# Attention scores of both heads of a pair together, as three float32r products of split queries and keys

## The chip, the core and the metric

The kernel runs on one core of one Trainium2 chip. The metric is the device time of one execution in microseconds (us). The core's engines work side by side, each through its own list in order: TensorE (PE) multiplies matrices into PSUM, VectorE (DVE) and ScalarE (ACT) do elementwise work and read PSUM, GpSimd (POOL) does elementwise work in SBUF, and SyncE (SP) issues the DMA transfers. Semaphores hold them together.

## The reference

Attention with a position bias made by a small network, for 2 batches, 8 heads, 576 positions and 64 columns a head; then two feed-forward layers over the 1152 rows of 512 columns.

```python
scores = scale * np.matmul(q, k.transpose(0, 1, 3, 2))      # scale = 1/8
x = (log1p(|i - j|) / log1p(max(i, 1)))[..., None]
bias = np.maximum(x @ w1 + b1, 0.0) @ w2                    # hidden 32, one column per head
scores = scores + bias.transpose(2, 0, 1)[None]
attn = softmax(scores)                                      # over the last axis
x = (attn @ v), heads side by side: (1152, 512)
h = x @ w_in;  x = (h * np.clip(h + 3.0, 0.0, 6.0) / 6.0) @ w_out       # d_ff 2048
xn = x / sqrt(mean(x * x) + 1e-06) * rms_g
x = (silu(xn @ w_gate) * (xn @ w_val)) @ w_out2                         # d_ff 1536
```

## The kernel before

**Tiles and units.** The 1152 query rows are nine tiles of 128. Eight tiles lie in one batch each; the seventh (`COMB`) holds the last 64 rows of both batches. A tile has four units `u`, one for each pair of heads, so there are 36 units; unit `u` is pair `u % 4` of tile `u // 4`.

**A unit.** `scores` (L418) is called once for each head `a` of the pair. Keys and queries lie transposed with 64 columns of a head on 64 partitions, even positions of the keys in the upper row half and odd ones in the lower half, and the queries are there twice, so a head is two fp32 matmuls of 128 queries by 288 keys (`L427`), one on each row half, into the two banks of one PSUM tile `s`. (The combined tile takes 64 queries for each batch: four matmuls.) The profile has two records for each fp32 matmul, the order one. `softmax_d` (L441, VectorE) adds the bias and takes the maximum `m`; `softmax_a` (L452, ScalarE) does the exponential. `e_turn` transposes the weights `e` in three parts, four, four and one blocks, on PE (`tps`), `e_copy` (L472) copies each part from PSUM to `et`, and `pv` (L490) multiplies with the values, ten fp32 matmuls. Once a tile the sums are inverted (`ri`), spread (`rb`), transposed (`rps`) and copied (`rt`, L514); `xf` (L519) applies them, and `xh` (a rounding to float32r, L528) and `xl` (what is left, L526) are the two parts that the feed-forward phases read. `k_copy` (L315) and `q_copy` (L325) bring transposed keys and queries from PSUM to SBUF.

**Bias.** It depends on the position alone. For each of 36 groups of 16 rows, `bias_R` (L344, L339) makes four tiles `R`, `bias_mm` (L357) contracts them on PE (`bps`), `bias_evac` brings them to `ev`, and `bias_store` (L387) writes them to DRAM; `bias_load` (L413, L410) reads a unit's bias back shifted, once the eight groups of its rows are stored. The groups are spread over the first twenty units or so.

**Feed-forward.** Weights, activations and normed rows are split into a float32r part and the rest, and every product is three float32r matmuls (`PASS`): L701 for the first product, L746 for the second. A weight is loaded by SP into `raw`, and turned into its two parts by ScalarE (`wm`, `wh`), VectorE (L138, L139, L143) and GpSimd (`wl`), one step a turn. A first few are converted while attention still runs, into `nb` early slots.

**What sets the order.** Each piece of work has a key, a number in units of `u`, made from `PARAMS`; the pieces are emitted in the order of their keys. Those up to key `man` keep that order on each engine; the later ones go through a scheduler, which orders each engine's list within what buffers and dependences allow. `START`, `MID`, `ET`, `KE` and `RB, RT, XH, XL` say on which engine (P, A, D) a copy is done. `BUFS` has the number of buffers of each pool: the score tiles `s` have two of two PSUM banks each, which wide bias products use too (L348). In the feed-forward part the order is the program's.

## Time and profile before

| | us |
|---|---|
| median of 3 runs (lowest to highest) | 662.5 (660.59 to 663.89) |
| the profiled execution | 662.26 |
| its span | 660.5 |
| busy: PE, VectorE, ScalarE, GpSimd | 633.3, 479.8, 342.6, 144.7 |

The span is what the trace shows; the profiled execution's own time has some 1.8 us around it. Busy time is the union of an engine's instructions, and matmuls are pipelined, so a PE that is busy all the time need not be at its peak; a share over the whole span is a mean of stages with different limits. In the trace attention ends at 218.2 us, where the first feed-forward matmul starts.

### The profile page before, as it was taken

The page shows a single profiled execution, that of the slowest core. Times are in us where ns is not written, and L with a number is a line of the kernel's source. Part 1 is how long each engine was busy: PE and PEld are TensorE (multiplying, and loading weights), DVE is VectorE, ACT ScalarE, POOL GpSimd, SP SyncE. Part 2 cuts the span into 40 slices and gives each one's busy share as a digit, 9 for nine tenths or more (in the row PEclk, how much of TensorE's full clock was granted, in tenths as well). Part 3 has the DMA queues.
Part 4 walks back from the last instruction along what each step waited for, and adds up shares of the span by engine and source line. Part 5 has one row for each costly group of instructions (what it writes and reads, how often), then busy time and mean ns, then how long its engine had stood idle before and what let it go on. Part 6 is the DMA issues. An engine that isn't in the chain of part 4 may idle for free.

```text
span 660.5 us, 11012 instructions
## 1 busy us (share of the span) xinstructions
PE 633.3 (96%) x4174; PEld 525.0 (79%) x4174; DVE 479.8 (73%) x885; ACT 342.6 (52%) x675; POOL 144.7 (22%) x117
## 2 busy tenths in 40 slices
...
GB/s 153 282 287 239 266 164 261 131 80 204 140 3 1 55 139 133 127 126 126 128 64 1 33 96 128 143 149 129 153 160 65 79 114 1 63 153 230 34 0 49
DMA packets 75250, 80.69 MB, mean 122 GB/s; under 512 B 23996, under 2 KB 59964, under 8 KB 75196
## 3 DMA queue, kind: packets, MB, share of 16 engines
...
q8 instruction: 33, 0.54, 0.3%
...
## 4 chain that ended last, share of the span: by engine, by line
PE 80%; DVE 11%; DMA 3%; issue 3%; ACT 1%; SPq 1%; DVEq 0%; ACTq 0%
PE h L701 33%; PE ya L746 16%; PE yb L746 8%; PE pv L490 6%; PE tps L86 6%; PE s L427 6%; PE bps L357 4%; DVE wm L139 2%; DVE e L441 1%; DVE wm L143 1%; DVE wm L138 1%; DMA bias<-biasd 1%; PE qps L86 1%; DMA raw<-in_moe_w_out_dram 1%; DVE R L344 1%
## 5 line engine op out<-in xcount | busy, mean ns | idle before, releaser
L151 POOL TENSOR_TENSOR wl<-wm,wh 128x512 fp32r<-128x512 f32 x86 | 126.4, 1470 | 301.1 <-ACT wh L122 176.2
L143 DVE SCALAR_TENSOR_TENSOR wm<-raw,wm 128x512 int32<-128x512 int32 x86 | 127.5, 1482 | 0.9
L710 ACT CAST gh<-r 128x384 fp32r<-128x384 f32 x84 | 43.2, 514 | 118.0 <-DVE r L733 71.2
L701 PE MATMUL h<-nh,wh 128*128 128x384 f32 x288 | 97.6, 339 | 5.1 <-DVE r L733 3.2
L701 PE MATMUL h<-nh,wl 128*128 128x384 f32 x288 | 96.7, 336 | 0.0
L701 PE MATMUL h<-nl,wh 128*128 128x384 f32 x288 | 96.5, 335 | 0.0
L441 DVE CUSTOM_DVE_ANT_1 e<-s,bias 128x576 f32<-128x576 f32 x72 | 54.3, 755 | 29.8 <-PE tps L86 17.7
L733 DVE TENSOR_TENSOR r<-r,h 128x384 f32<-128x384 f32 x36 | 19.9, 551 | 66.6 <-PE h L701 66.3
L452 ACT ACTIVATE e<-e,m 128x576 f32<-128x576 f32 x72 | 56.0, 778 | 19.8 <-DVE m L441 19.8
L701 PE MATMUL h<-xh,wh 128*128 128x384 f32 x192 | 65.4, 341 | 0.0
L701 PE MATMUL h<-xh,wl 128*128 128x384 f32 x192 | 64.7, 337 | 0.0
L139 DVE SCALAR_TENSOR_TENSOR wm<-raw,wm 128x512 int32<-128x512 int32 x86 | 62.5, 727 | 2.9
L701 PE MATMUL h<-xl,wh 128*128 128x384 f32 x192 | 64.4, 336 | 0.0
L701 PEld LDWEIGHTS h<-nh,wh 128*128 128x128 f32 x288 | 54.1, 188 | 8.6 <-DVE r L733 4.0
L130 ACT ACTIVATE wm<-raw 128x512 f32<-128x512 f32 x86 | 58.0, 674 | 5.1 <-DMA raw<-in_moe_w_in_dram 2.2
L713 DVE TENSOR_TENSOR gl<-r,gh 128x384 fp32r<-128x384 f32 x84 | 46.6, 554 | 15.6 <-ACT gh L710 15.6
L427 PE MATMUL s<-kS,q 64*128 64x288 f32 (+1 forms) x320 | 54.6, 449 | 2.7 <-DVE m L441 2.7
L86 PEld LDWEIGHTS tps<-ident,e 128*128 128x128 f32 x324 | 42.5, 200 | 18.2 <-issue 8.9
L86 PE MATMUL tps<-ident,e 128*128 128x128 f32 x324 | 55.9, 297 | 0.1
L344 DVE TENSOR_SCALAR R<-T,NB 128x368 f32<-128x368 f32 (+17 forms) x124 | 54.0, 485 | 2.2 <-PE bps L357 1.7
L122 ACT CAST wh<-wm 128x512 fp32r<-128x512 f32 x86 | 52.9, 617 | 4.7 <-DVE wm L143 4.7
L701 PEld LDWEIGHTS h<-nl,wh 128*128 128x128 f32 x288 | 54.1, 188 | 1.4
...
## 6 DMA issues: line engine op xcount, KB each, us to landing
...
```

Source lines behind the costliest of these rows:

```text
L86: nc.tensor.transpose(out, in_, ident[:n, :n])
L122: nc.scalar.copy(out=hi, in_=m)
L130: nc.scalar.activation(out=m, in_=raw[:, :, 1].bitcast(F32), func=ACTF.Abs, scale=2.0 ** -112)
L139: nc.vector.scalar_tensor_tensor(out=m, in0=raw[:, :, 0], scalar=29, in1=m, op0=ALU.logical_shift_right, op1=ALU.bitwise_or,)
L143: nc.vector.scalar_tensor_tensor(out=m, in0=raw[:, :, 1], scalar=-0x80000000, in1=m, op0=ALU.bitwise_and, op1=ALU.bitwise_or,)
L151: nc.gpsimd.tensor_tensor(out=lo, in0=m, in1=hi, op=ALU.subtract)
L344: nc.vector.tensor_scalar(out=R, in0=src, scalar1=NB1[:, col], scalar2=None, op0=ALU.max)
L427: nc.tensor.matmul(s[sl, r, :SH], lhsT=q_t[t][h // 4][rows, h % 4, sl], rhs=kS[b][rows, h, :], start=True, stop=True,)
L441: nc.vector.tensor_tensor_reduce(out=e_t[u][:, a, :].rearrange("p (j r) -> p r j", r=2), in0=s[:, :, :SH], in1=bt[u][:, a, :].rearrange("p ...
L452: nc.scalar.activation(out=e_t[u][:, a, :], in_=e_t[u][:, a, :], func=ACTF.Exp, scale=-1.0, bias=m_t[t][:, h:h + 1], accum_out=sum_t[t][:, ...
L701: nc.tensor.matmul(ps, lhsT=w[wz][:, c * 128:(c + 1) * 128], rhs=x[xz][:, c, :], start=(i == 0), stop=(i == 11),)
L746: nc.tensor.matmul(y_t[ph, n, t], lhsT=g[gz][:, t * 128:(t + 1) * 128], rhs=w[wz], start=(f == 0 and i == 0), stop=(f == F - 1 and i == 2),)
```

## The change

Keys and queries are each split into a float32r part (`h`) and the rest (`l`), on the way out of PSUM: `k_part` and `q_part` take the places of `k_copy` and `q_copy`, once for the high part (the engine of before, now a cast) and once for the low part (VectorE: a subtraction that reads PSUM again). A score is three products, high by high, high query by low key, low query by high key, which add up in PSUM. `scores` is called once a unit and emits both heads. In the combined tile the queries of each batch get tiles of their own with zeros in the other batch's 64 columns, so that all matmuls have 128 queries and both batches add into one tile: twelve matmuls a head. The numbers in `PARAMS` move keys: bias groups come closer together (`gr` 1.076 to 1.163), bias loads are asked earlier (`bl` -3.209 to -5.532), one block of k is asked 2.3 units earlier (`k4` -0.333 to -2.61), the values of both batches are loaded closer together (`lv0`, `lv1`), and `kl` and `ql`, 0.1 and 0.3 units, set the low parts behind the high ones. The engine strings move copies: for each fourth unit the first part-1 copy of `et` and for each fourth the one-block copy go from VectorE to ScalarE, `rt` and `xh` too, and `xl` goes from GpSimd to VectorE. Six early weight slots stand in place of eight, nine `R` buffers in place of eleven, three `ev` in place of four. `far` has the value that stood in the code.

```diff
--- before.py
+++ after.py
@@ -27,22 +27,22 @@
-    g0=-5.972, gs=0.601, g8=-0.524, gt=-0.138, g14=1.055, gr=1.076, man=-0.96, zra=-0.531, zrd=-0.393, zrp=-1.107,
+    g0=-5.972, gs=0.601, g8=-0.524, gt=-0.138, g14=1.055, gr=1.163, man=-0.96, zra=-0.643, zrd=-0.393, zrp=-1.107,
...
 START = ["DDDD", "DDAA", "DDAD", "DDDA", "DDDD", "DDDA", "DDDA", "DDDD"]
 MID = ["DDDD", "DDDA"]
-ET = ["DADA", "DAAA", "DDDD"]
+ET = ["DADA", "AAAA", "DADD"]
 KE = ["D", "D"]
-RB, RT, XH, XL = "PDDP"
-SLOTS = dict(wr=3, na=0, nb=8, ns=29)
-BUFS = dict(rawk=4, rawq=2, qp=2, bp=5, ep=2, etp=3, sm=3, Rp=11, evp=4, xa=1, ps_s=2, ps_t=3, ps_v=1)
+RB, RT, XH, XL = "PAAD"
+SLOTS = dict(wr=3, na=0, nb=6, ns=29, far=60)
+BUFS = dict(rawk=4, rawq=2, qp=2, bp=5, ep=2, etp=3, sm=3, Rp=9, evp=3, xa=1, ps_s=2, ps_t=3, ps_v=1)
 
 
 @with_exitstack
@@ -80,6 +80,9 @@
 
     xh = [xp.tile([128, 4, BT], F32R, tag=f"xh{n}", name=f"xh{n}") for n in range(NB)]
     xl = [xp.tile([128, 4, BT], F32R, tag=f"xl{n}", name=f"xl{n}") for n in range(NB)]
+
+
+    PASS = ((0, 0), (0, 1), (1, 0))
 
     def transpose(out, in_):
         n = in_.shape[0]
@@ -247,7 +250,7 @@
         ps_v = actx.enter_context(tc.tile_pool(name="ps_v", bufs=BUFS["ps_v"], space=PSUM))
 
 
-        kS = [p.tile([128, H, SH], F32, name=f"kS{b}") for b, p in enumerate((kp0, kp1))]
+        kS = [[p.tile([128, H, SH], F32R, name=f"kS{b}{z}") for z in "hl"] for b, p in enumerate((kp0, kp1))]
         vs = [p.tile([128, 2, H, 2, D], F32, name=f"vs{b}") for b, p in enumerate((vp0, vp1))]
 
         v4 = [p.tile([128, 4, 2, D], F32, name=f"v4{b}") for b, p in enumerate((vp0, vp1))]
@@ -304,25 +307,40 @@
         def k_turn(x):
             ps_of["k", x] = turn_four(raw_t["k", *x], "kps")
 
-        def k_copy(x, z, engine):
+        def k_part(x, z, lower, engine):
             b, blk, hh = x
             if blk == 2:
                 src = ps_of["k", x].rearrange("p h (b y c) -> p b y h c", b=2, y=2)[:, z]
-                dst = kS[z][:, :, 256:288].rearrange("p (y h) c -> p y h c", y=2)
+                hi, lo = [a[:, :, 256:288].rearrange("p (y h) c -> p y h c", y=2) for a in kS[z]]
             else:
                 src = ps_of["k", x]
-                dst = kS[b][:, 4 * hh:4 * hh + 4, 128 * blk:128 * blk + 128]
-            copy(engine)(out=dst, in_=src)
+                hi, lo = [a[:, 4 * hh:4 * hh + 4, 128 * blk:128 * blk + 128] for a in kS[b]]
+            if lower:
+                nc.vector.tensor_tensor(out=lo, in0=src, in1=hi, op=ALU.subtract)
+            else:
+                copy(engine)(out=hi, in_=src)
 
         q_t = {}
 
         def q_turn(t, hh):
             ps_of["q", t, hh] = turn_four(raw_t["q", t][:, 4 * hh:4 * hh + 4], "qps")
 
-        def q_copy(t, hh):
-            if hh == 0:
-                q_t[t] = [qp.tile([128, 4, 128], F32, tag=f"q{z}", name=f"q{z}") for z in range(2)]
-            nc.scalar.activation(out=q_t[t][hh], in_=ps_of["q", t, hh], func=ACTF.Copy, scale=0.125)
+        def q_alloc(t, hh):
+            nb = 2 if t == COMB else 1
+            q_t[t, hh] = [[qp.tile([128, 4, 128], F32R, tag=f"q{hh}{z}", name=f"q{hh}{z}") for z in "hl"] for b in range(nb)]
+            if t == COMB:
+                for b in range(2):
+                    for z in range(2):
+                        nc.vector.memset(q_t[t, hh][b][z][:, :, 64 * (1 - b):64 * (1 - b) + 64].bitcast(F32), 0.0)
+
+        def q_part(t, hh, b, lower):
+            sl = slice(64 * b, 64 * b + 64) if t == COMB else slice(0, 128)
+            src = ps_of["q", t, hh][:, :, sl]
+            hi, lo = [a[:, :, sl] for a in q_t[t, hh][b]]
+            if lower:
+                nc.vector.scalar_tensor_tensor(out=lo, in0=src, scalar=0.125, in1=hi, op0=ALU.mult, op1=ALU.subtract)
+            else:
+                nc.scalar.activation(out=hi, in_=src, func=ACTF.Copy, scale=0.125)
 
 
         R_t = {}
@@ -415,24 +433,27 @@
 
         e_t, sum_t, m_t = {}, {}, {}
 
-        def scores(u, a):
+        def scores(u):
 
             t, p = divmod(u, 4)
-            h = 2 * p + a
-            s = ps_s.tile([128, 2, 512], F32, tag="s", name="s")
-            cols = [(0, slice(0, 64)), (1, slice(64, 128))] if t == COMB else [(TILES[t][0], slice(0, 128))]
-            for b, sl in cols:
-                for r in range(2):
-                    rows = slice(64 * r, 64 * r + 64)
-                    nc.tensor.matmul(
-                        s[sl, r, :SH], lhsT=q_t[t][h // 4][rows, h % 4, sl], rhs=kS[b][rows, h, :], start=True, stop=True,
-                    )
-            if a == 0:
-                e_t[u] = ep.tile([128, 2, S], F32, tag="e", name="e")
-                if p == 0:
-                    sum_t[t] = sm.tile([128, H], F32, tag="sum", name="sum")
-                    m_t[t] = sm.tile([128, H], F32, tag="m", name="m")
-            ps_of["s", u, a] = s
+            ops = [(b, i) for b in range(2 if t == COMB else 1) for i in range(3)]
+            for a in range(2):
+                h = 2 * p + a
+                s = ps_s.tile([128, 2, 512], F32, tag="s", name="s")
+                for y, (b, i) in enumerate(ops):
+                    qz, kz = PASS[i]
+                    kk = kS[b if t == COMB else TILES[t][0]][kz]
+                    for r in range(2):
+                        rows = slice(64 * r, 64 * r + 64)
+                        nc.tensor.matmul(
+                            s[:, r, :SH], lhsT=q_t[t, h // 4][b][qz][rows, h % 4, :], rhs=kk[rows, h, :],
+                            start=(y == 0), stop=(y == len(ops) - 1),
+                        )
+                ps_of["s", u, a] = s
+            e_t[u] = ep.tile([128, 2, S], F32, tag="e", name="e")
+            if p == 0:
+                sum_t[t] = sm.tile([128, H], F32, tag="sum", name="sum")
+                m_t[t] = sm.tile([128, H], F32, tag="m", name="m")
 
         def softmax_d(u, a):
             s = ps_of["s", u, a]
@@ -599,7 +620,8 @@
             at(-99 + i if i < 3 else key + P["lk"], ("lk", x), (), (lambda *x: None) if i < 2 else load_k, *x)
             at(key + P[w + "kt"], ("kT", x), [("lk", x)], k_turn, x)
             for z in range(B) if blk == 2 else [b]:
-                at(key + P[w + "kt"] + P[w + "kc"], ("kC", x, z), [("kT", x)], k_copy, x, z, KE[i % 2])
+                at(key + P[w + "kt"] + P[w + "kc"], ("kh", x, z), [("kT", x)], k_part, x, z, 0, KE[i % 2])
+                at(key + P[w + "kt"] + P[w + "kc"] + P[w + "kl"], ("kC", x, z), [("kh", x, z)], k_part, x, z, 1, "D")
         at(P["lv0"], ("lv", 0), (), load_v, 0)
         at(P["lv1"], ("lv", 1), (), load_v, 1)
         QK = {(0, 0): P["q0"], (0, 1): P["q1"], (1, 0): P["q2"], (1, 1): P["q3"]}
@@ -609,17 +631,20 @@
                 w = "z" if (t, hh) == (0, 0) else ""
                 key = QK.get((t, hh), 4 * (t - 1) + (P["qa"], P["qb"])[hh])
                 at(key, ("qT", t, hh), [("lq", t, hh)], q_turn, t, hh)
-                at(key + P[w + "qh"], ("qP", t, hh), [("qT", t, hh)], q_copy, t, hh)
+                at(key, ("qA", t, hh), (), q_alloc, t, hh)
+                for b in range(2 if t == COMB else 1):
+                    at(key + P[w + "qh"], ("qh", t, hh, b), [("qA", t, hh), ("qT", t, hh)], q_part, t, hh, b, 0)
+                    at(key + P[w + "qh"] + P[w + "ql"], ("qP", t, hh, b), [("qh", t, hh, b)], q_part, t, hh, b, 1)
         for u in range(NU):
             t, p = divmod(u, 4)
             c = 4 if t == COMB else TILES[t][1]
             at(max(u + P["bl"], stored_key[c] + .001 * (1 + u % 4)), ("bl", u), [("ST", n) for n in range(8 * c, min(8 * c + 8, NG))], bias_load, u)
             ks = [("kC", (b, blk, p // 2), b) for b in (range(B) if t == COMB else [TILES[t][0]]) for blk in range(2)]
             ks += [("kC", (0, 2, 0), b) for b in range(B)]
+            at(u + P["s0"], ("S", u), ks + [("qP", t, p // 2, b) for b in range(2 if t == COMB else 1)], scores, u)
             for a in range(2):
                 x = "01"[a]
-                at(u + P["s" + x], ("S", u, a), ks + [("qP", t, p // 2)], scores, u, a)
-                at(u + P["d" + x], ("D", u, a), [("S", u, a), ("bl", u)], softmax_d, u, a)
+                at(u + P["d" + x], ("D", u, a), [("S", u), ("bl", u)], softmax_d, u, a)
                 at(u + P["e" + x], ("E", u, a), [("D", u, a)], softmax_a, u, a)
             for part in range(3):
                 x = "012"[part]
@@ -688,8 +713,6 @@
         y_t, x_t = {}, {}
         for n in range(NB):
             x_t[0, n] = (xh[n], xl[n])
-        HP = 100
-        PASS = ((0, 0), (0, 1), (1, 0))
 
         def first(kind, ph, n, f):
             w = slot_of[kind, f]
@@ -871,7 +894,7 @@
                     x = turn.pop(0)
                     norm_6(*x, norm_5(*x))
                 late_step()
-                while len(pend) < 3 and weight_want(i + 1 - len(queue), 8, 60):
+                while len(pend) < 3 and weight_want(i + 1 - len(queue), 8, 60 if ph == 0 else SLOTS["far"]):
                     pass
             for x in queue:
                 finish(*x)
```

**The order, PE, near the end of attention** (units 32 to 34; `tps` are transposes of `e`, `s` score tiles, `pv` the products with v). Before:

```order
L86 MATMUL tps_2571<-ident_63,e_2455 128x128 x4
L86 MATMUL tps_2578<-ident_63,e_2505 128x128 x4
L427 MATMUL s_2583<-kS1_139,q1_2302 128x288 x2
L86 MATMUL tps_2590<-ident_63,e_2505 128x128
L427 MATMUL s_2592<-kS1_139,q1_2302 128x288 x2
L490 MATMUL pv_2604<-et_2550,vs1_141 64x128 x8
L490 MATMUL pv_2604<-et_2550,v41_143 64x128 x2
```

After:

```order
L89 MATMUL tps_2950<-ident_63,e_2815 128x128 x4
L89 MATMUL tps_2957<-ident_63,e_2875 128x128 x4
L89 MATMUL tps_2966<-ident_63,e_2875 128x128
L511 MATMUL pv_2987<-et_2929,vs1_143 64x128 x5
L448 MATMUL s_2968<-kS1h_140,q1h_2854 128x288 x2
L448 MATMUL s_2968<-kS1l_141,q1h_2854 128x288 x2
L448 MATMUL s_2968<-kS1h_140,q1l_2855 128x288 x2
L448 MATMUL s_2975<-kS1h_140,q1h_2854 128x288 x2
L448 MATMUL s_2975<-kS1l_141,q1h_2854 128x288 x2
L448 MATMUL s_2975<-kS1h_140,q1l_2855 128x288 x2
L511 MATMUL pv_2987<-et_2929,vs1_143 64x128 x3
L511 MATMUL pv_2987<-et_2929,v41_145 64x128 x2
```

The two score runs with a transpose between them have become one run of both heads, the nine transposes stand together, and the products with v stand in two pieces on both sides of the scores (in other units in one).

**The order, VectorE, at the start** (`R` are the bias group's tiles; the row of 384 columns that ends each list is the last R of the eighth group, or holds it). Before:

```order
L315 COPY kS_138<-kps 128x4x128
L344 TENSOR_SCALAR R<-T,NB_116 128x336
L344 TENSOR_SCALAR R<-T,NB_116 128x368
L344 TENSOR_SCALAR R<-T,NB_116 128x352
L315 COPY kS_138<-kps 128x8x32
L315 COPY kS_139<-kps 128x8x32
L344 TENSOR_SCALAR R<-T,NB_116 128x368
L344 TENSOR_SCALAR R<-T,NB_116 128x384
L344 TENSOR_SCALAR R<-T,NB_116 128x368
L344 TENSOR_SCALAR R<-T,NB_116 128x384 x3
```

After:

```order
L321 CAST kS0h<-kps 128x8x32
L321 CAST kS1h<-kps 128x8x32
L319 TENSOR_TENSOR kS0l<-kps,kS0h 128x8x32
L319 TENSOR_TENSOR kS1l<-kps,kS1h 128x8x32
L362 TENSOR_SCALAR R<-T,NB_116 128x368
L341 SCALAR_TENSOR_TENSOR q0l<-qps,q0h 128x512
L362 TENSOR_SCALAR R<-T,NB_116 128x384
L362 TENSOR_SCALAR R<-T,NB_116 128x368
L362 TENSOR_SCALAR R<-T,NB_116 128x384 x2
L321 CAST kS0h<-kps 128x4x128
L319 TENSOR_TENSOR kS0l<-kps,kS0h 128x4x128
L362 TENSOR_SCALAR R<-T,NB_116 128x384
```

The low parts of k and q stand among the R rows, and one more block of k (high and low) has moved ahead of the last of them.

## Rows read from the trace of the kernel before

**Rows 1.** Windows by stage: window, length, busy us (instructions) of each engine, PEclk, DMA share.

```profile
0.00:32.30 32.30, 19.84 (x150) 8.19 (x150) 21.21 (x65) 21.56 (x42) 2.60 (x15) 1.00 0.79 216
32.30:52.50 20.20, 17.92 (x145) 11.05 (x146) 17.12 (x44) 12.22 (x27) 0.64 (x1) 1.00 0.98 283
52.50:141.60 89.10, 87.71 (x840) 55.33 (x843) 76.74 (x191) 62.80 (x128) 8.00 (x8) 1.00 0.69 195
...
81.80:98.90 17.10, 16.13 (x155) 9.98 (x154) 17.10 (x43) 11.33 (x23) 2.09 (x2) 1.00 0.56 161
...
179.70:218.20 38.50, 38.50 (x406) 28.65 (x405) 22.03 (x59) 22.60 (x49) 3.34 (x4) 1.00 0.01 2
218.20:655.20 437.00, 431.91 (x2231) 396.37 (x2232) 317.64 (x467) 197.43 (x375) 122.60 (x83) 1.00 0.32 99
```

**Rows 2.** Chain of waits, first feed-forward phase: start us, us, what.

```profile
224.62 2.08 PE ya L746 x9
226.70 2.10 PE h L701 x12
```

**Rows 3.** Chain of waits in the last units of attention.

```profile
193.68 0.69 PE s L427 x4
194.37 0.26 PE tps L86
194.63 0.69 PE s L427 x4
...
196.56 1.15 PE tps L86 x8
...
198.98 0.11 PE tps L86
```

**Rows 4.** Timelines of ScalarE, SP and VectorE at the start: start us, us, what [idle before].

```profile
21.26 1.10 ACT L381 ACTIVATE ev<-bps,cc,INV 128x384 f32<-128x384 f32 x2
...
22.05 1.74 SPq L283 DMA_DIRECT2D rawk<-in_k_dram  x1
23.88 3.23 SPq L387 DMA_DIRECT2D biasd<-ev  x3
...
32.30 0.76 DVE L441 CUSTOM_DVE_ANT_1 e<-s,bias 128x576 f32<-128x576 f32 x1 [4.02 <-DMA bias<-biasd]
```

**Rows 5.** Timeline of PE in the combined tile.

```profile
162.78 0.71 PE L427 MATMUL s<-kS,q 64*64 64x288 f32 x8
163.42 0.33 PE L86 MATMUL qps<-ident,rawq 128*128 128x128 f32 x1
```

**Rows 6.** Groups by form up to 218.2 us: count | busy us, mean ns | idle before.

```profile
L472 DVE COPY et<-tps 128x512 f32<-128x512 f32 x27 | 18.5, 686 | 0.2 <-PE tps L86 0.2
L472 DVE COPY et<-tps 128x128 f32<-128x128 f32 x36 | 10.3, 286 | 2.6 <-PE tps L86 2.6
...
L519 DVE TENSOR_TENSOR xf<-pv,rt 128x512 f32<-128x512 f32 x8 | 5.5, 690 | 5.1 <-PE pv L490 4.7 <-issue 0.4
...
L528 DVE CAST xh<-xf 128x512 fp32r<-128x512 f32 x8 | 3.8, 472 | 0.0
...
L472 ACT COPY et<-tps 128x512 f32<-128x512 f32 x45 | 25.6, 585 | 30.6 <-PE tps L86 30.6
```

**Rows 7.** Waits: up to 218.2 us; from 32; from 218.2 (total us, times, longest).

```profile
DVE e L441 <- DMA bias<-biasd: 5.4, 2, 4.0
...
PE s L427 <- DVE m L441: 2.7, 4, 1.2
...
PE h L701 <- DVE r L733: 3.2, 2, 1.7
```

**Rows 8.** Timelines of PE's weight loads (PEld) and matmuls (PE) within a score run.

```profile
153.52 0.19 PEld L427 LDWEIGHTS s<-kS,q 64*128 64x128 f32 x2
...
153.52 0.30 PEld L427 LDWEIGHTS s<-kS,q 64*128 64x128 f32 x4
...
153.52 0.51 PE L427 MATMUL s<-kS,q 64*128 64x288 f32 x2
```

10 lines of the change are left out of this document (5 added, 5 removed).

## The prediction

> **What bounds the kernel now.** I read the windows by stage first, then the chain of waits, then the groups by form for VectorE (DVE) and ScalarE (ACT). From 218.2 us on, the two feed-forward phases fill TensorE (PE): 431.9 of 437.0 us busy [rows 1], in runs of twelve 128x384 matmuls in 2.10 us and nine 128x512 in 2.08 us without a gap [rows 2]. The change leaves those instructions alone, so what it is worth must come out of the first 218.2 us. Of these the last 38.5 us (units 28 to 35, a unit being one pair of heads of one query tile; there are 36) are PE from end to end, with VectorE at 22.0 and ScalarE at 22.6 [rows 1]; the chain there is score run, one transpose, score run, then products with v, eight transposes, and round again [rows 3]. From 52.5 to 141.6 us it is mostly PE too, 87.7 of 89.1 us, but VectorE is close behind: between 81.8 and 98.9 us VectorE is busy for the whole 17.10 us and PE for 16.13 [rows 1]. Before 52.5 us PE is not the limit: it is busy 19.8 of 32.3 and 17.9 of 20.2 us [rows 1], and the first softmax keeps VectorE waiting 4.02 us for a bias tile that was stored to DRAM and comes back [rows 4].
>
> **What one score run costs.** A head's run is four records (two row halves, two records each) and the next work starts 0.69 us later; four records in turn would not fit, so the halves run side by side. A lone transpose between two score runs takes 0.26 us, and 0.11 us where it follows other transposes; eight that follow a run of another kind take 1.15 us, so 0.27 more than eight times 0.11 [rows 3]. Starting and ending a run therefore costs 0.15 to 0.27 us, and I take 0.2. That leaves 0.49 us for the reading of 288 columns in fp32. The float32r matmuls of the feed-forward part give the new price: 2.10/12 for 384 columns and 2.08/9 for 512 [rows 2], both 0.13 us for 288. Three products are 0.39 us per head where the halves still run side by side, a gain of 0.10 us. No row has a float32r matmul on half the rows, so the ends are: 0.12 us a pair and a run cost of 0.15 (0.54 to 0.36, a gain of 0.18), and 0.13 with a run cost of 0.27 (0.42 to 0.39, a gain of 0.03). For the 64 plain heads that is -6.4 us (-11.5 to -1.9).
>
> The combined tile (four units, the rest rows of both batches) loses. Its eight records now fill four quarters of the array and end after 0.64 us [rows 5], so 0.44 without the run cost. With zeros in the unused half, each head needs six pairs, 0.78 us: +0.34 for 8 heads, +2.7 us (with 0.12 a pair +2.2).
>
> **Runs.** The change emits both heads together, which would leave 36 score runs. The built order does not get there. Up to the first feed-forward matmul I count 71 score runs before and 54 after, 81 and 66 runs of transposes, but 39 and 57 of the products with v and 27 and 31 of bias products, since the score tiles still share two PSUM buffers with the wide bias products and the scheduler cuts the v products in two to fill in. In all 219 runs become 209: -10 x 0.2 = -2.0 us. So the score runs fall, and most of that is given back in split v products. PE in sum: -6.4 + 2.7 - 2.0 = -5.7 us, of which the eight heads of the first four units (0.8) lie where PE isn't the limit: **-4.9 us**.
>
> **VectorE, early.** Ten low parts of k are new (eight at 0.69, the price of the product at L519 that reads PSUM at the same width, and two of half the size at about 0.4: 6.3 us), and sixteen low parts of q with four half-size ones (12.6 us) and eight clears (under 0.3 each, like a 128-column copy: 2 us) [rows 6]. The high part of k stands where its copy stood. What leaves VectorE: nine copies et of 512 columns (6.2) and nine of 128 (2.6), nine copies rt of 512 (6.2) and eight casts xh (3.8) [rows 6]; eight subtractions xl come over from GpSimd at 0.69 (5.5). Net it gains some 8 us in the first 218.2, and the gain stands early: 9.1 us (all ten of k, four of q) before the end of unit 3. In the order, two whole low parts of k, two half-size ones and one of q (2.9 us), and one more pair of k (1.4), stand ahead of the last R of the eighth bias group, whose store the first bias load waits for. Before the change ScalarE had evacuated that group at 22.36 us, SP was held by a k load from 22.05 to 23.79, and the store went out at 23.88; VectorE then had nothing to do for 4.02 us until the bias came [rows 4]. So part of the 4.3 us is hidden by the lateness of ScalarE and SP, and other low parts fall into the idle 4.02. I take +1.3 us to the first softmax and +1.2 for what is left until unit 4: **+2.5 us**, between 0 (the idle time holds it all) and +9.1 (none of it).
>
> **VectorE and stalls, later.** Per unit its work falls in the stretch where it was full, because nine wide and nine narrow copies move to ScalarE. PE's missing 0.97 us of 81.8 to 98.9 and the 2.7 us that four score runs waited for a maximum m [rows 1, 7] should mostly go: all four weight conversions that VectorE does in attention stood ahead of the combined tile, and now they stand in it or behind it. I take **-2.0 us** (0 to -4).
>
> **ScalarE** receives nine wide copies, nine narrow, nine rt and eight xh: about 18 us at the 585 ns of a 512-column copy [rows 6] and half of that for the narrow ones. It is busy 22.6 of 38.5 us in the last stretch and 62.8 of 89.1 from 52.5 to 141.6 [rows 1], so I cost it at nothing; PE's work hides it. If it doesn't, the transposes' copies come late and v products wait: 0 to +4 us.
>
> Edits at nothing: six in place of eight early weight slots, fewer R and ev buffers, and one conversion less in the third feed-forward unit cost a lead, not time, as long as weights stay ahead; PE waited 3.2 us in two places for r in the whole feed-forward part and for no weight [rows 7]. Bias loads are asked earlier on SP; a load that waits for its buffer holds up q loads and stores behind it, but q tiles are also asked earlier and softmax waited for a DMA just twice, both times at the start [rows 7].
>
> **Sum.** The profiled execution took 662.26 us, of which 660.5 is the span; the median of the three runs is 662.5, so the two can stand for each other. 662.3 - 4.9 + 2.5 - 2.0 = 657.9, forecast **658 us**.
>
> **Rivals.**
> (a) All fits: the good ends. Score heads -11.5 with 1.4 of it lost early, combined tile +2.2, runs -2.0, no early cost, stalls -4: 662.3 - 13.9 = 648 us. For it speaks that the last 38.5 us are nothing but PE; against it that VectorE was busy 17.1 of 20.2 us right after its idle spell.
> (b) The gain is eaten: ScalarE's 18 us and the two shared score buffers make PE wait as long as it now waits for columns (+4): 662 us. For it: ScalarE already runs at seven tenths with the exponentials on it.
> (c) Slower, by VectorE early: the low parts delay the R rows, so the eighth store, so the first bias load, and the idle 4.02 us move with them rather than take them in. All 9.1 us go on the path and the stalls stay: 662.3 - 4.9 + 9.1 = 666.5 us. It decides from the point at which the R rows, not ScalarE's evacuation and SP's queue, are the last before that store.
> (d) Slower, by loading: each pair's weights wait until the pair before on the same row half has ended. A load is 0.11 us (two loads end after 0.19, all four after 0.30) [rows 8]; a pair would be 0.24, a head 0.72 in place of 0.49: 64 x 0.23 = +14.7 with 1.8 of it early, the combined tile 8 x (1.44 - 0.44) = +8, runs -2, and +2.5 and -2: 682 us. Against it: the third and fourth load, on the same halves as the first two, are over at 0.30 us after the run's start, while the first two matmuls last to 0.51 [rows 8]. The Trainium skill, "TensorE: Matmul & The Clock Gate", Part 3 (The mechanism), states that "LDWEIGHTS overlaps with in-flight MATMULs only when row_grp differs"; by that rule (d) would hold. The trace disagrees for these fp32 runs, as the rows just named show.
>
> **How the numbers follow.** Forecast and its neighbourhood (654 to 662) 0.50; (a) 0.15; (b) 0.20; (c) 0.09; (d) 0.06. A measurement of this kernel tells about 0.5% from no change, 3.3 us, so the borders are 659 and 665.6. Of the forecast's half I put 0.30 below 659. Faster 0.30 + 0.15 = 0.45; same 0.20 + 0.20 = 0.40; slower 0.15. The range leaves out (d) and about half of (a): 649 to 667.
>
> **What would show it.** Right: score runs of six records in about 0.6 us or twelve in about 1.0; pairs start 0.13 us apart; the last eight units in 35 us or less; the first softmax at 33 to 35 us; the feed-forward part still 437 us. Wrong: pairs 0.24 us apart (d); the first softmax at 37 us or later, or unit 4 after 57 (c); idle PE before score runs, released by m, or before v products, released by ScalarE's et (b); a wait for a weight in the feed-forward part, for which no term stands here.

## The result and the profile after

| | before | after |
|---|---|---|
| median, us (lowest to highest of 5) | 661.35 (660.59 to 663.89) | 666.91 (666.17 to 669.83) |
| the profiled execution, its span | 662.26, 660.5 | 666.91, 665.1 |
| first softmax; first softmax of unit 4 | 32.3; 52.5 | 33.4; 58.0 |
| first feed-forward matmul | 218.2 | 222.8 |

The kernel became slower: the ratio is 1.0081, 95% interval 1.0059 to 1.0102, some 5.5 us where 4.3 us less had been forecast. The direction was wrong; that the time lies inside the range, by 0.1 us, is luck. An execution more than 1.5% above the fastest of its kernel counts as slow and stays out of every ratio below; the only one is the profiled execution of e10 (676.33 us), and no time is read from its trace.

The windows by stage of the kernel after (window, length, busy us and instructions of PE, PEld, DVE, ACT and POOL, PEclk, DMA share, GB/s) answer [rows 1]. The third lies within the second.

```profile
0.00:33.40 33.40, 20.51 (x154) 7.83 (x154) 25.26 (x72) 20.14 (x39) 2.61 (x15) 1.00 0.84 213
33.40:58.00 24.60, 23.03 (x163) 15.22 (x167) 19.47 (x48) 15.12 (x34) 0.65 (x1) 0.79 0.97 278
36.00:46.00 10.00, 9.39 (x47) 6.27 (x45) 7.83 (x21) 5.39 (x12) 0.00 (x0) 0.50 0.93 286
58.00:146.80 88.80, 88.80 (x922) 61.29 (x917) 69.78 (x180) 68.03 (x143) 2.30 (x4) 1.00 0.56 151
146.80:165.90 19.10, 17.75 (x190) 14.79 (x190) 14.03 (x38) 12.37 (x30) 0.83 (x2) 1.00 0.85 191
165.90:186.00 20.10, 19.17 (x254) 16.73 (x254) 13.95 (x34) 13.14 (x30) 0.62 (x1) 1.00 0.78 245
186.00:222.80 36.80, 36.61 (x431) 30.60 (x429) 22.53 (x58) 28.45 (x63) 4.47 (x4) 1.00 0.05 16
222.80:659.80 437.00, 431.94 (x2232) 396.41 (x2232) 316.94 (x467) 197.93 (x375) 122.30 (x83) 1.00 0.31 99
```

Two stages of the kernel before that [rows 1] leaves out, units 20 to 23 and the combined tile:

```profile
141.60:162.40 20.80, 19.63 (x182) 12.98 (x176) 13.53 (x31) 15.18 (x32) 5.16 (x4) 1.00 0.68 168
162.40:179.70 17.30, 17.30 (x230) 12.31 (x230) 10.59 (x29) 10.44 (x24) 2.31 (x3) 1.00 0.59 166
```

The feed-forward part takes 437.0 us as before, so the whole difference is made in attention. Stage by stage: first softmax +1.1 us; units 0 to 3 +4.4 (24.6 for 20.2); units 4 to 19 -0.3 (88.8 for 89.1); units 20 to 23 -1.7; the combined tile +2.8 (20.1 for 17.3); units 28 to 35 -1.7. The sum is +4.6: +5.5 up to unit 4 and -0.9 from there on, where TensorE's busy time fell by 0.8 us (163.1 to 162.3). In units 0 to 3 the granted clock is 0.50 for ten microseconds, 1.2 GHz in place of 2.4.

The score runs do what they should. The timeline of TensorE in one run of both heads (start us, us, what; answers the gaps of [rows 8]), then the chain of waits around it (answers [rows 3]):

```profile
196.03 0.40 PE L448 MATMUL s<-kS0h,q1h 64*128 64x288 f32 x2
196.27 0.29 PE L448 MATMUL s<-kS0l,q1h 64*128 64x288 f32 x2
196.41 0.29 PE L448 MATMUL s<-kS0h,q1l 64*128 64x288 f32 x2
196.54 0.30 PE L448 MATMUL s<-kS0h,q1h 64*128 64x288 f32 x2
196.67 0.29 PE L448 MATMUL s<-kS0l,q1h 64*128 64x288 f32 x2
196.80 0.29 PE L448 MATMUL s<-kS0h,q1l 64*128 64x288 f32 x2
```

```profile
194.04 1.26 PE tps L89 x9
195.30 0.80 PE pv L511 x9
196.10 0.99 PE s L448 x12
197.09 0.80 PE pv L511 x10
197.89 1.26 PE tps L89 x9
```

Pairs start 0.13 us apart, on the same two row halves, and the run of both heads is 0.99 us in the chain where two runs of 0.69 stood. But the products with v stand on both sides of it, 0.80 us twice. Sorting all matmuls of attention by what they write, with the time from a matmul's start to the next one's start less the gaps in which none runs, gives:

```
us (runs)   tps        s          pv         bps        all    idle
before      50.6 (76)  49.9 (71)  46.8 (39)  33.4 (27)  201.1   9.6
after       49.8 (66)  45.6 (54)  53.0 (57)  36.3 (31)  206.1   9.4
e1          51.2 (68)  42.5 (42)  46.3 (36)  34.2 (28)  195.1  17.3
e9          49.5 (68)  44.5 (53)  52.7 (57)  33.6 (30)  200.4  10.7
e11         50.9 (71)  41.7 (41)  46.4 (39)  33.7 (28)  192.8  16.9
e14         50.9 (68)  42.4 (43)  46.3 (38)  35.1 (29)  195.7  14.3
```

(The last four rows are experiments, below. The table is summed from the matmul records of the traces.) The scores lost 4.3 us and the products with v gained 6.2, 0.34 us for each of 18 more runs. Ten microseconds at half clock stretch the row of the changed kernel. e9 has the same score and product runs within one, at full clock (0.999 in the mean): there the scores lost 5.4 us, the products with v gained 5.9, and all matmuls together lost 0.7.

### The profile page after: what moved, and what is told of

It is laid out like the page before. It is cut to its first block, busy times and chain, and to the rows that moved or that the text cites. A ratio compares the mean times of both kernels' runs of the same rounds, so it can differ in the third digit from the quotient of the medians.

```text
span 665.1 us, 11422 instructions
## 1 busy us (share of the span) xinstructions
PE 638.3 (96%) x4334; PEld 543.0 (82%) x4334; DVE 483.0 (73%) x896; ACT 355.6 (53%) x712; POOL 133.8 (20%) x109
## 4 chain that ended last, share of the span: by engine, by line
PE 83%; DVE 7%; DMA 3%; issue 3%; ACT 2%; SPq 1%; DVEq 0%; ACTq 0%
PE h L724 33%; PE ya L769 16%; PE yb L769 8%; PE pv L511 7%; PE tps L89 7%; PE s L448 6%; PE bps L375 4%; DVE wm L142 2%; DVE wm L146 1%; DVE wm L141 1%; PE qps L89 1%; PE kps L89 1%; DMA biasd<-ev 1%; DMA bias<-biasd 1%; DVE gl L736 1%
## 5 line engine op out<-in xcount | busy, mean ns | idle before, releaser
L146 DVE SCALAR_TENSOR_TENSOR wm<-raw,wm 128x512 int32<-128x512 int32 x86 | 126.4, 1469 | 0.9
L462 DVE CUSTOM_DVE_ANT_1 e<-s,bias 128x576 f32<-128x576 f32 x72 | 51.9, 756 | 19.1 <-PE tps L89 16.8
L142 DVE SCALAR_TENSOR_TENSOR wm<-raw,wm 128x512 int32<-128x512 int32 x86 | 61.6, 716 | 3.0
L724 PEld LDWEIGHTS h<-nh,wh 128*128 128x128 f32 x288 | 54.1, 188 | 8.6 <-DVE r L756 4.0
L744 ACT ACTIVATE r<-h,half_c 128x384 f32<-128x384 f32 x48 | 27.8, 580 | 51.7 <-PE h L724 51.7
L89 PEld LDWEIGHTS tps<-ident,e 128*128 128x128 f32 x324 | 42.5, 201 | 15.5 <-issue 6.5
L724 PEld LDWEIGHTS h<-nl,wh 128*128 128x128 f32 x288 | 54.1, 188 | 1.4
L724 PEld LDWEIGHTS h<-nh,wl 128*128 128x128 f32 x288 | 54.0, 188 | 0.0
```

What stands on the lines that cost most here:

```text
L89: nc.tensor.transpose(out, in_, ident[:n, :n])
L142: nc.vector.scalar_tensor_tensor(out=m, in0=raw[:, :, 0], scalar=29, in1=m, op0=ALU.logical_shift_right, op1=ALU.bitwise_or,)
L146: nc.vector.scalar_tensor_tensor(out=m, in0=raw[:, :, 1], scalar=-0x80000000, in1=m, op0=ALU.bitwise_and, op1=ALU.bitwise_or,)
L462: nc.vector.tensor_tensor_reduce(out=e_t[u][:, a, :].rearrange("p (j r) -> p r j", r=2), in0=s[:, :, :SH], in1=bt[u][:, a, :].rearrange("p ...
L724: nc.tensor.matmul(ps, lhsT=w[wz][:, c * 128:(c + 1) * 128], rhs=x[xz][:, c, :], start=(i == 0), stop=(i == 11),)
```

## Experiments

Three causes were in sight at first: the split products with v (theory A), the clock in units 0 to 3 (B), ScalarE's new copies near the end (C). Each run was measured beside the kernel before on the same chip; ratios carry their 95% interval. Seventeen kernels ran.

| run | base | median, us | ratio to before |
|---|---|---|---|
| e1 whole products with v | after | 665.83 | 1.0056 (1.0042 to 1.0070) |
| e2 clock held | after | 668.21 | 1.0095 (1.0082 to 1.0108) |
| e3 copies back | after | 670.80 | 1.0127 (1.0111 to 1.0143) |
| e4 new numbers alone | before | 671.39 | 1.0142 (1.0129 to 1.0155) |
| e5 split alone | after | 671.60 | 1.0164 (1.0131 to 1.0196) |
| e6 heads apart | after | 666.32 | 1.0073 (1.0057 to 1.0089) |
| e7 one product | after | 652.39 | 0.9864 (0.9847 to 0.9881) |
| e8 fewer buffers alone | before | 668.53 | 1.0108 (1.0092 to 1.0125) |
| e9 buffers back | after | 663.33 | 1.0044 (1.0021 to 1.0066) |
| e10 three ev alone | before | 672.28 | 1.0126 (1.0083 to 1.0169) |
| e11 e1 and e9 | after | 663.26 | 1.0028 (1.0017 to 1.0039) |
| e12 e4 with old buffers | before | 666.77 | 1.0087 (1.0072 to 1.0102) |
| e13 e11, high k on ScalarE | after | 662.21 | 1.0017 (1.0007 to 1.0028) |
| e14 e13, some R on ScalarE | after | 661.85 | 1.0009 (1.0000 to 1.0018) |
| e15 e13, more R on ScalarE | after | 666.76 | 1.0086 (1.0072 to 1.0099) |
| e16, e17 e14, clock held | after | 662.03, 662.06 | 1.0011 (1.0000 to 1.0022), 1.0019 (1.0007 to 1.0032) |

**e1, the products with v in one piece.** In both `pv` and `scores` the first matmul of a call is bound behind what was written before it (`b_` counts the batches).

```diff
-    nc.tensor.matmul(pv_t[t][64 * a:64 * a + 64, p, sl], lhsT=lhsT, rhs=rhs, start=(x == 0), stop=(x == 4))
+    one = nc.tensor.matmul(pv_t[t][64 * a:64 * a + 64, p, sl], lhsT=lhsT, rhs=rhs, start=(x == 0), stop=(x == 4))
+    if x + a + b_ == 0:
+        tc.keep_in_program_order(one)
...
+                        one = nc.tensor.matmul(
                             s[:, r, :SH], lhsT=q_t[t, h // 4][b][qz][rows, h % 4, :], rhs=kk[rows, h, :],
...
+                        if a + y + r == 0:
+                            tc.keep_in_program_order(one)
```

> The first product with v of a unit and the first score matmul of a unit are each bound, in TensorE's order, behind what the program wrote before them. The products with v then stand in 36 pieces in place of 57, the score runs are 42 in place of 54, all runs together 204 in place of 240. Theory A, the split products: in the changed kernel the products with v take 54.1 us of TensorE's time against 47.0 before, with 18 more pieces, 0.39 us each; whole again, they fall back to 46 to 48 us, score runs save 12 x 0.2 = 2.4 us more, and the time comes to 657 to 660 us. Rival, the order is not the cause: TensorE then stands still before the scores (both score buffers taken until the maximum is there) for what it saves, the products fall but the idle time before s and pv grows by as much, 665 to 668 us.

The products fell to 46.3 us and the scores to 42.5, eleven microseconds of TensorE less in all, as theory A asks. (The expectation's 54.1 and 47.0 us count the gaps too.) The time fell by 1 to 2 us, with intervals that overlap, and idle time rose from 9.4 to 17.3 us, as the rival asks. Windows by stage of e1, units 0 to 3, 4 to 19, 20 to 23, the combined tile and units 28 to 35:

```profile
32.70:57.90 25.20, 20.54 (x167) 13.65 (x171) 19.82 (x49) 14.97 (x33) 0.65 (x1) 0.86 0.98 277
57.90:145.80 87.90, 85.88 (x922) 59.92 (x923) 69.46 (x181) 68.76 (x144) 2.51 (x4) 1.00 0.58 149
145.80:163.90 18.10, 16.57 (x190) 14.14 (x189) 13.89 (x37) 12.14 (x29) 0.78 (x2) 1.00 0.88 210
163.90:184.00 20.10, 18.50 (x255) 16.23 (x254) 13.92 (x35) 13.07 (x31) 0.62 (x1) 1.00 0.80 237
184.00:219.70 35.70, 35.31 (x430) 29.83 (x428) 22.96 (x58) 28.04 (x63) 4.81 (x4) 1.00 0.04 11
```

TensorE is now idle for 4.7 of 25.2 us in units 0 to 3, and they are no shorter: unit 4 starts at 57.9 us (58.0 in the changed kernel). From there on it is otherwise: 161.8 us in place of 164.8, with 6.1 us less of TensorE's work. So half of the saving came through from unit 4 on, and next to none before it. The run binds TensorE's order as well as joining the pieces, so part of the new idle time can be the binding's own; that wasn't separated.

**e2, the clock.** Ten dummy matmuls of 512 columns stand behind early bias products.

```diff
+        def warm():
+            ps = ps_v.tile([128, 4, 128], F32, tag="v", name="wps")
+            nc.tensor.matmul(ps.rearrange("p a b -> p (a b)")[:, :512], lhsT=ident, rhs=T[:, :512], start=True, stop=True)
...
+            if 4 <= i < 14:
+                at(g + P[z + "b"] + .0001, ("warm", n), [("B", n)], warm)
```

> Ten dummy matmuls of 512 fp32 columns (about 0.9 us each, into a PSUM bank that is free then) stand behind the bias products of the groups 5 to 14, where TensorE is idle for over a third of the time between 22 and 34 us. Theory B, the clock: in the changed kernel the granted clock is 0.5 (1.2 GHz) from 35.8 to 46.0 us, and TensorE is busy 9.39 of the 10 us there; with the clock at 1.0 in that stretch up to 4.5 us come back, less 1 us at most for dummies in the way: 662 to 664 us, and units 0 to 3 take 20 to 21.5 us in place of 24.6. Rival: those units are held by VectorE, which does low parts of k and q there, and by loads; then the clock reads 1.0 and units 0 to 3 still take 23.5 us or more, 666 to 668 us.

Units 0 to 3 of e2:

```profile
34.00:58.40 24.40, 23.12 (x191) 14.22 (x187) 20.04 (x48) 15.37 (x34) 0.00 (x0) 1.00 0.99 278
```

The clock reads 1.00 throughout and the stretch still takes 24.4 us; the time is 1.3 us above that of the changed kernel. Two of the ten dummies, 2.2 us, lie within these units, so this run alone doesn't rule the clock out. The changed kernel's own executions say more: at mean clocks of 0.996 and 0.997, as high as in most executions of the kernel before, two of the five took 666.33 and 666.17 us, 5 us above the kernel before. The low clock is not what makes up the loss.

**e3, the copies back.**

```diff
-ET = ["DADA", "AAAA", "DADD"]
+ET = ["DADA", "DAAA", "DDDD"]
-RB, RT, XH, XL = "PAAD"
+RB, RT, XH, XL = "PDDP"
```

> Only the copies go back to the engines of before: the part-1 and one-block copies of et of each fourth unit, rt and xl, xh (VectorE, VectorE, GpSimd, VectorE), with the key distance of that copy. Theory C: ScalarE's moved copies cost time in the last units, where it is busy 28.5 of 36.0 us and for 5 us carries the chain; without them units 28 to 35 take 34.5 to 35 us in place of 36.8 and the time is 664 to 665.5 us. Rival: the moved copies pay, VectorE with the low parts is fuller without them (17 us more in attention), units 4 to 19 take 90 us or more in place of 88.8 and the time is 667 to 671 us.

(One key, `c1`, the distance of that copy, goes back too.) Slower by 4 us than the changed kernel, and units 28 to 35 take 38.2 us in place of 36.8, not less: theory C falls. With the low parts on VectorE, the copies are better on ScalarE.

**e4, the other half alone:** the kernel before with all new numbers, strings, slots and buffer counts.

> The other half of the change alone: the kernel before with its fp32 scores, head by head, but with all new numbers, engine strings, slots and buffer counts. If the loss comes from the moved copies and the new keys (theory C and others), it shows here without any split of k and q: 665 to 668 us. If it comes from the split and the joined scores (theories A and B), this kernel is within 1.5 us of the one before, 660 to 663 us, and its granted clock stays at 1.0 up to 50 us.

This alone costs 9.5 us, more than either expectation, with no split and no joined scores. The clock had been expected to stay at 1.0 if the split was to blame; it falls here without it. Units 0 to 3 of e4:

```profile
32.80:61.30 28.50, 26.48 (x143) 14.33 (x147) 15.85 (x41) 14.46 (x32) 0.65 (x1) 0.76 0.92 256
```

**e5, the split alone:** the changed code with the old keys and strings (`PARAMS`, `ET`, `RB, RT, XH, XL` of before), only the buffer counts and early slots those of the change.

> Split keys and queries and joined score runs as in the changed kernel, with all keys and engine strings of the kernel before; only the buffer counts stay those of the change (nine R, three ev, six early slots), since the low parts fill the memory. In the kernel with the new numbers alone the granted clock fell to 0.5 between about 42 and 55 us and units 0 to 3 took 28.6 us. Theory D, the new numbers bring the loss of the first units: here the clock stays at 1.0, units 0 to 3 take 20 to 22 us and the time is 658 to 662 us. Rival, the split itself brings it and the new numbers were fitted to it: units 0 to 3 take 25 us or more, and with VectorE's copies of before the time is 668 to 673 us.

The time is the rival's. The new keys were no gift to the old kernel (e4), yet the new code needs them: without them it is 5 us worse than with them. What e4 and e5 share is the counts of R and ev tiles, and the six early slots.

**e6, heads apart:** `scores(u, a)` once for each head, at keys `s0` and `s1` again, three products each.

> The changed kernel with the scores of each head called apart, at the two keys of before, three float32r products each. In the order the products with v stand in 45 pieces in place of 57, but the score runs are 78 in place of 54 and the transposes 77 in place of 66, 261 runs in place of 240. Theory A, what counts is the number of runs: 21 more at 0.2 to 0.39 us make 4 to 8 us, 670 to 674 us. Rival, joining the heads is what hurts, since both score buffers are asked for at once: 662 to 665 us, with the products with v at 49 us.

Neither expectation holds: 666.32 us is the changed kernel's time. The score runs are 78, the products with v 48.1 us in 45 runs, TensorE's work 202.9 us, and the granted clock 1.00 in units 0 to 3. What joining saved in score runs it lost in split products, no more.

**e7, one product:**

```diff
-            ops = [(b, i) for b in range(2 if t == COMB else 1) for i in range(3)]
+            ops = [(b, i) for b in range(2 if t == COMB else 1) for i in range(1)]
```

> The changed kernel with the first product alone: the two low products of each score are left out, and the low parts are still made. Two pairs of 0.13 us fewer for each of 64 heads are 16.6 us, four of six pairs for 8 heads of the combined tile 4.2 us, 20.8 us of TensorE. If TensorE is what limits attention, 646 to 649 us. If the chain of scores, maximum, exponential and copies limits it (the rival, for which the 10 us of idle TensorE in the kernel with whole products speak), less than half comes out: 656 to 663 us, and TensorE's idle time grows by the rest.

14.5 us came out of 20.8 taken away, between the two theories. The products with v now stand in 76 pieces and take 56.6 us, so that TensorE's work fell by 17.8 us only, and some eight tenths of that reach the time: where the order is left free, most of a saving of TensorE in attention counts here. The combined tile falls from 20.1 to 16.1 us.

**e8 and e10, fewer buffers alone,** both on the kernel before:

```diff
-BUFS = dict(rawk=4, rawq=2, qp=2, bp=5, ep=2, etp=3, sm=3, Rp=11, evp=4, xa=1, ps_s=2, ps_t=3, ps_v=1)
+BUFS = dict(rawk=4, rawq=2, qp=2, bp=5, ep=2, etp=3, sm=3, Rp=9, evp=3, xa=1, ps_s=2, ps_t=3, ps_v=1)
```

(e8; in e10 `Rp` stays 11 and only `evp` is 3.)

> The kernel before with nothing changed but two buffer counts: nine R tiles in place of eleven and three ev tiles in place of four, which is what the low parts' memory takes. The forecast costed this at nothing. If that holds: 660.5 to 663.5 us. Theory E, the buffers are the price of the first units: ScalarE's evacuation waits for a store to end (2.6 us between 20 and 58 us before, 4.5 in the changed kernel), so the PSUM tile of the bias comes free late, TensorE waits, and the time is 664 to 668 us with units 0 to 3 at 22 us or more.

> The kernel before with three ev tiles in place of four and its eleven R tiles: half of the run with fewer buffers. If the ev tiles, which wait for a store to end, are the price: 666 to 669 us. If the R tiles are: 661 to 663 us.

Nothing but two numbers changed, and the kernel before is 1.08% slower; with the ev tiles alone 1.26%. So the ev tiles have a price. Whether the R tiles have one too is open: at mean clocks of 0.995 and 0.996 e10 took 666.03 and 664.62 us and e8 668.12 and 667.18, while the rest of e10 ran at 0.987 and less. The rows tell where it comes in. SP's list between 22 and 58 us, first of the kernel before, then of e8 (start us, us, what; "idle" is what lies between one row's end and the next row's start):

```profile
33.68 1.33 SPq L387 DMA_DIRECT2D biasd<-ev  x1
36.22 2.32 SPq L273 DMA_DIRECT2D rawq<-in_q_dram  x2
38.59 2.91 SPq L291 DMA_DIRECT2D vs<-in_v_dram  x2
...
52.57 3.35 SPq L387 DMA_DIRECT2D biasd<-ev  x4
```

```profile
35.34 0.87 SPq L283 DMA_DIRECT2D rawk<-in_k_dram  x1
41.60 0.52 SPq L387 DMA_DIRECT2D biasd<-ev  x1
42.18 1.15 SPq L291 DMA_DIRECT2D vs<-in_v_dram  x2
```

In e8 SP stands from 36.2 to 41.6 us before the store of a bias group, the fourteenth, and the loads of v, which started at 38.59 before, start at 42.18. ScalarE's evacuations of that group, before, then in e8 (there with the next group's):

```profile
30.37 0.48 ACT L381 ACTIVATE ev<-bps,cc,INV 128x144 f32<-128x144 f32 x1
...
31.20 0.75 ACT L381 ACTIVATE ev<-bps,cc,INV 128x447 f32<-128x447 f32 x1
```

```profile
40.51 2.04 ACT L381 ACTIVATE ev<-bps,cc,INV 128x144 f32<-128x144 f32 x4
```

With four tiles the fourteenth group was evacuated ahead of the first exponential (33.10 us) and its store went out at 33.68, ahead of the loads of v. With three it needs the tile of the eleventh group, which is stored at 31.50 us in e8, and it stands in ScalarE's list behind the first exponentials; its store, on SP, still stands ahead of the loads of v. The waits between 18 and 58 us say on whom (who, for whom: us in total, times, longest), before, then e8:

```profile
ACT ev L381 <- DMA biasd<-ev: 2.6, 3, 1.6
SPq L387 <- ACT ev L381: 1.6, 3, 0.9
```

```profile
ACT ev L381 <- DMA biasd<-ev: 2.9, 5, 1.3
SPq L387 <- ACT ev L381: 11.0, 7, 5.3
```

ScalarE itself hardly waits longer for stores (2.9 us for 2.6); SP's longest wait, 5.3 us, ends with the group's late place in ScalarE's list. In all SP waits 11.0 us for evacuations in place of 1.6, with k, q and v loads behind. TensorE then waits for v in e8 (`pv`, 0.97 and 0.33 us idle at 50 us) and reaches unit 4 at 56.2 us. The changed kernel has the same mark, and evacuates the fourteenth group at 41.50 us:

```profile
36.06 0.72 SPq L294 DMA_DIRECT2D vs<-in_v_dram  x1
42.61 0.53 SPq L405 DMA_DIRECT2D biasd<-ev  x1
```

```profile
ACT ev L399 <- DMA biasd<-ev: 4.5, 5, 1.6
SPq L405 <- ACT ev L399: 9.9, 6, 5.7
```

**e9, the buffers back in the changed kernel,** paid for by one raw k tile and one bias tile:

```diff
-BUFS = dict(rawk=4, rawq=2, qp=2, bp=5, ep=2, etp=3, sm=3, Rp=9, evp=3, xa=1, ps_s=2, ps_t=3, ps_v=1)
+BUFS = dict(rawk=3, rawq=2, qp=2, bp=4, ep=2, etp=3, sm=3, Rp=11, evp=4, xa=1, ps_s=2, ps_t=3, ps_v=1)
```

> The changed kernel with eleven R and four ev tiles again; the memory comes from raw k tiles (three in place of four) and bias tiles (four in place of five). Fewer R and ev tiles cost the kernel before 7.3 us. Theory E: here a good part comes back, units 0 to 3 take 21 to 22.5 us in place of 24.6, ScalarE's wait for stores falls from 4.5 us to 3 or less, and the time is 661 to 664 us. Rival: the new numbers were fitted to the fewer buffers, and the tiles given up (k loads later, bias loads held by a buffer) cost as much: 665.5 to 670 us.

663.33: 3.6 us back by the medians, two thirds of the loss, from memory that was lying elsewhere. By the ratios (1.0081 to 1.0044) it is 2.4 us, since three of its twelve executions, at mean clocks of 0.985 to 0.992, took 666.9 to 670.1 us; the four at 0.997 took 662.1 to 664.1, where the changed kernel at 0.997 took 666.2. Its waits, and its windows from the first softmax on:

```profile
ACT ev L399 <- DMA biasd<-ev: 2.2, 3, 1.1
SPq L405 <- ACT ev L399: 3.3, 5, 1.1
```

```profile
32.00:53.50 21.50, 18.43 (x159) 12.25 (x163) 19.22 (x48) 13.00 (x30) 0.65 (x1) 1.00 1.02 291
53.50:142.30 88.80, 88.80 (x923) 61.34 (x916) 70.19 (x183) 68.87 (x145) 2.45 (x4) 1.00 0.58 152
142.30:161.40 19.10, 17.72 (x191) 14.77 (x190) 14.01 (x38) 12.37 (x30) 0.75 (x2) 1.00 0.76 180
161.40:181.70 20.30, 19.23 (x254) 16.72 (x253) 13.90 (x34) 13.44 (x30) 0.61 (x1) 1.00 0.90 261
181.70:218.40 36.70, 36.51 (x429) 30.53 (x428) 22.52 (x58) 28.44 (x63) 4.46 (x4) 1.00 0.08 28
```

The first softmax comes at 32.0 us, units 0 to 3 take 21.5 in place of 24.6, and what follows is as long as in the changed kernel (164.9 and 164.8 us to the first feed-forward matmul). The fourteenth group is evacuated at 30.59 us, and the loads of v start at 38.78. So with the buffers back all but 1.0 us of what was lost before unit 4 is gone (53.5 for 52.5), and nothing changes after it. In these two executions the clock differs too (1.00 in units 0 to 3, 0.79 in the changed kernel), and its part in the 4.5 us isn't separated.

**e11, e1 and e9 together.**

> Both repairs: the order of the run with whole products with v (39 pieces here, 41 score runs, 209 runs in all) and the buffers of the run before last. If the idle 10 us of TensorE in the kernel with whole products come from the late bias (theory E), they shrink to 6 or 7 us and the time is 657 to 661 us. If they come from the chain through VectorE and ScalarE (the order waits where it used to fill in), the time stays at 664 to 667 us.

663.26, the same as e9. TensorE works 192.8 us, 8 less than before the change, and is idle for 16.9. The time lies between the two expectations, but the idle time did not shrink (17.3 in e1), so the late bias was not what made it.

**e12, the new keys and strings on the kernel before, with its own buffers.**

> The kernel before, fp32 scores and all, with the new numbers and engine strings but eleven R and four ev tiles (six early slots): the run with the new numbers alone was 9.5 us slower, the run with fewer buffers alone 7.3 us. Theory E: what is left without the buffers is 1 to 4 us, 662 to 665 us. Rival, keys and strings carry a loss of their own: 667 us or more, with the clock at 0.5 between 40 and 55 us as in the run with all new numbers.

4.6 us better than e4, which the buffers take, and 5.3 us worse than before, which keys, strings and early slots take on the fp32 kernel (the clock reads 0.74 over units 0 to 3 here too). The expectation's border of 667 was met almost exactly; both theories hold in part.

**e13, e14, e15, VectorE's load in the first units.** On e11: six of nine high parts of k from ScalarE; then, besides, one R tile of four of the ninth to sixteenth bias group; then two of four of the ninth to fourteenth.

```diff
-                at(key + P[w + "kt"] + P[w + "kc"], ("kh", x, z), [("kT", x)], k_part, x, z, 0, KE[i % 2])
+                at(key + P[w + "kt"] + P[w + "kc"], ("kh", x, z), [("kT", x)], k_part, x, z, 0, "A" if i > 2 else "D")
...
-            R_eng[n] = START[i] if i < 8 else MID[i % len(MID)]
+            R_eng[n] = START[i] if i < 8 else "DDDA" if i < 16 else MID[i % len(MID)]
```

(e14 has both, e13 the first alone; e15 has `"DDAA" if i < 14` in the second.)

> The run with whole products and the buffers back, and six of the nine k blocks (all but the three first) get their high part from ScalarE in place of VectorE. In that run VectorE is full from 31 to 45 us, with the casts and low parts of k and q among the R tiles and the first softmaxes, ScalarE only 14.0 of 23.6 us, and units 0 to 3 take 23.6 us against 20.2 before. Theory F, VectorE's part of the split is what holds the first units: without 4 us of casts they take 20.5 to 22 us, and the time is 660 to 662 us. Rival, not VectorE but the PSUM tiles that the low parts keep occupied, or the late bias: 23 us or more, 662.5 to 665 us.

> As the run before it in this list, and one of the four R tiles of each of the ninth to sixteenth bias group from ScalarE, where every second group has one now: four R tiles, 1.7 us, more off VectorE. Theory F: 0.5 to 1.5 us better than the run without it. Rival: ScalarE's evacuations of the bias become late, PE waits for ev 2 us more, the time is the same or up to 2 us worse.

> The same with two of four R tiles of the ninth to fourteenth group on ScalarE: nine tiles, 3.8 us, off VectorE. Theory F: units 0 to 3 at 20 to 21 us, the time 659 to 661 us. Rival, ScalarE takes VectorE's place as the engine that is full from 31 to 45 us: 23 us or more, 663 us or more.

By the medians e13 gained 1.1 us, between its two expectations, and e14 a little more; e15 lost 4.6 against e13. That is its rival's number, but not its mechanism: ScalarE is busy 10.8 of the 15 us from 30 to 45, and the clock is low in two spells (0.63 from 30 to 35 us, 0.55 from 40 to 45). Windows of e11 (31.2) and e14 (33.0) over units 0 to 3:

```profile
31.20:54.80 23.60, 18.52 (x167) 12.59 (x171) 20.54 (x50) 14.02 (x32) 0.65 (x1) 1.00 1.04 299
```

```profile
33.00:53.30 20.30, 19.44 (x142) 12.58 (x140) 16.13 (x42) 16.64 (x38) 0.65 (x1) 0.83 0.99 288
```

With VectorE and ScalarE even (16.1 and 16.6 us), these units take 20.3 us, as before the change. But the first softmax comes 1.8 us later than in e11, and units 4 to 19 take 90.1 us in place of 88.2: unit 20 starts at 143.4 us in e14 and at 143.0 in e11. The profiled executions show no gain (661.75 and 661.23 us); the medians show 1.4 us. That VectorE's parts of k and q hold the first units is therefore not shown. e14 ties with the kernel before (1.0009); no run with all three products beat it.

**e16, e17, the clock once more,** on e14, with nine dummies of 256 and ten of 128 columns.

> The kernel of the run before this (whole products, buffers back, high parts of k and one R of each early group on ScalarE) with nine dummy matmuls of 256 fp32 columns, about 0.45 us each, behind the bias products of the groups 4 to 12, where TensorE waits. In that run the granted clock was 0.5 from about 34.5 to 40.5 us with TensorE busy all that time, so up to 3 us hang on it. Theory B, the clock: it stays at 1.0 up to 55 us and the time is 659.5 to 661 us. Rival: the dummies stand in the way as they did in the changed kernel (1.5 to 3 us) and take what the clock gives: 661.5 to 664 us.

> The same with ten dummies of 128 columns, half the length (0.23 us each, 2.3 us in all). If they hold the clock too, they cost half as much as the 256-column ones: 659 to 660.5 us. If they don't, the clock falls as without them and the time is 661.5 to 663 us.

Units 0 to 3 of e16 and, within them, the 8 us in which e14 ran mostly at the low clock; then the same 8 us of e14:

```profile
33.20:53.20 20.00, 17.41 (x139) 11.06 (x139) 16.12 (x43) 16.29 (x37) 0.65 (x1) 1.00 1.09 301
34.00:42.00 8.00, 6.31 (x53) 4.42 (x53) 7.85 (x22) 6.92 (x16) 0.00 (x0) 1.00 1.04 375
```

```profile
34.00:42.00 8.00, 8.00 (x48) 5.16 (x49) 6.45 (x17) 5.93 (x15) 0.00 (x0) 0.59 1.02 343
```

At the full clock TensorE is busy 6.31 us of 8, with five more records than at the low one, where it was busy all 8; and the stage is 0.3 us shorter: the low clock had stretched work into waiting time. The time is the same with both lengths, and that of e14; the clock reads 1.00 in e17 too (34 to 55 us), so of its two expectations the one of a held clock misses by 1.6 us.

## Why the prediction was wrong

Two steps failed, one for the time before unit 4 and one for the time after it. Up to unit 4 the forecast had +2.5 us, and +5.5 was measured; from there on it had -6.9 (-4.9 and -2.0), and -0.9 was measured.

- **The first step that failed: "edits at nothing"**, and there "six in place of eight early weight slots, fewer R and ev buffers ... cost a lead, not time". The text looked for the price in weights of the feed-forward part, where indeed there is none (437.0 us both times). Fewer R and ev tiles cost the kernel before 1.08%, about 7 us (e8), and giving them back to the changed one brings 2.4 to 3.6 us, all of it before unit 4 (e9). [Rows 4] had the warning: a store on SP waits for an evacuation, with loads behind it.
- **The second: PE in sum, -5.7, with -4.9 on the path.** TensorE's work in attention fell by 0.7 us, not 5.7 (e9, at full clock). Pairs of 0.13 us were right, so rival (d), loads not overlapped, falls, and the count of runs was right; the price of a run was not. Scores: -5.4 in place of -7.1 (6.4 and 17 runs at 0.2, less 2.7). Products with v: +5.9 in place of +3.6, 0.33 us a run and not 0.2. Transposes: -1.5 in place of -3.0. That little saved work is little saved time shows in the stages: from unit 4 on TensorE was busy 0.8 us less, and the time was 0.9 us less. That a real saving counts there is shown by e7 (14.5 of 17.8 us) and, by half, by e1 (3.0 of 6.1).
- **The combined tile** met its number by luck: +2.8 us for +2.7. Its scores take 6.4 us in four runs where 5.2 stood in eight, +1.2; products with v in seven runs for four add 1.0, and idle time 0.9.
- **VectorE, early, +2.5.** The first softmax moved by +1.1 (+1.3 forecast), and its wait for the bias, 4.0 us in [rows 4], shrank:

```profile
DVE e L462 <- DMA bias<-biasd: 1.2, 2, 0.6
```

  That the size came out is luck too: with the buffers back and the same low parts the first softmax comes at 32.0 us, 0.3 earlier than before the change (e9). Unit 4 came at 58.0 us, past the 57 that had been named as the mark of rival (c), and the time, 666.9, is (c)'s 666.5. But (c)'s mechanism is a small part: in e9 unit 4 comes at 53.5, +1.0.
- **Stalls, -2.0.** They went (TensorE is busy 88.80 of 88.80 us in units 4 to 19, 87.7 of 89.1 before), and the split products took their place: these units took 0.3 us less.
- **ScalarE at nothing: not refuted.** Its copies pay (e3). Whether it comes near a limit of its own isn't shown.
- **The clock** had no term. In the profiled executions it fell in e4 and e12 too, where no low part exists, and stayed up in e6, e9 and e11. Held up, it brought nothing in e2, e16 and e17. Yet in e9 the slower executions are those with the lower mean clock (661.91 us at 1.000, 670.11 at 0.985), so it can have a price; which waits decide that isn't settled here.
- **The rest.** e14 stands 0.1% above before, with TensorE 5 us lighter and as much more idle. Which wait takes those 5 us wasn't isolated, nor what the bound order of e1, e11 and e14 adds to it; no kernel without the zeros of the combined tile ran.
